# A planned attention + experts + relu-squared kernel: GpSimd takes a multiplication of VectorE, and the planner gets new costs and a new table of due times

## The chip, the cores and the metric

The kernel runs on one core of one Trainium2 chip. The metric is the device time of one execution in microseconds (us), the median of three runs; lower is better. The engines are named as in the profile: PE (TensorE matmul), PEld (its weight loads), DVE (VectorE), ACT (ScalarE), POOL (GpSimd), SP (SyncE, which issues most DMAs).

## What is computed

Three layers follow each other. All inputs and outputs are float32.

```python
# attention: 2 batches, 8 heads, 576 positions, 64 wide; window of 128 back
scores = scale * np.matmul(q, k.transpose(0, 1, 3, 2))
bias = slopes[:, None, None] * (-np.abs(rel))[None, :, :]
scores = np.where(mask, scores + bias[None], -1e9)
attn = softmax(scores)                      # rows, with + 1e-09 in the divisor
x = np.matmul(attn, v)                      # then (1152, 512)
# four experts, weighted by the normalised domain probabilities
p = domain_probs / (domain_probs.sum(-1, keepdims=True) + 1e-09)
for e in range(4):
    out += p[:, e:e + 1] * (np.maximum(x @ w1[e], 0.0) @ w2[e])     # 512 -> 1024 -> 512
# a last layer
h = np.maximum(x @ w_in, 0.0)               # 512 -> 2048
return h * h @ w_out
```

## The kernel before

**Work and precision.** Most matmuls run on operands split in two: a rounded part (`xh`, `wh`, `qh`, `kh`) and the rest (`xl`, `wl`, `ql`, `kl`), three products in place of one. A rounding is a copy into the rounded type (`rounded`, L555 on ACT, L557 on DVE); a rest is a subtraction (`rest`, L561, on POOL or DVE).

**Units.** Attention is cut into units of two heads. The first four units (`u` 0 to 3, "raw") are the first 128 positions of both batches and use plain float32; later ones cover 256 or 192 positions of one batch. Each unit goes through a chain of stages named in the table of due times: `sc` (scores, PE L908/L922/L931), `jo` (join the mask, DVE L949), `mx` (add the bias, find the maximum, DVE L969), `ex` (exponential, ACT L979, four squares in a raw unit), `in` (sum and reciprocal, DVE L986 and L990), `no` (normalise, DVE L995, ACT L1002 or POOL L1008), `tp` (transpose, PE L1018), `hi` (copy out of PSUM, L555 or L557), `ow`/`be` (mask both halves, POOL L1039), and then `pv` (attention times v, PE L798 for the raw units, L812 later) and its evacuation: `evx` (raw units, into `xfirst`), `evh` and `evl` (rounded part and rest of `x`).

**First expert meanwhile.** The first expert's first product (`g1`: PE L1901 in plain float32 for the first positions, L1103 later) and second product (`g2`: L1852, L1343) are interleaved with the attention units, item by item, with the roundings and rests of its weights (`wh`, `wlo` in the table).

**What sets the order.** All of this up to about 120 us is a static plan. `Plan.add` records a task: the engines it may use with occupancy and latency, what it depends on, which buffers it takes, and a due time, to which the table `LATER` adds a number by the task's name. `Plan.run` then plays the tasks against a small model of five engines and emits them: it takes the engine that can start earliest, and of the tasks ready on it the one due first. The order in which it emits is the order of each engine's queue on the chip. The model charges an overlap of DVE and POOL: `HELD` lengthens the POOL side, `SLOWED` times the overlap lengthens a DVE task that is marked `shared`. Where PE would sit idle in the first microseconds, `keep_busy` (L588) fills the modelled gap with small matmuls on zeros, the `pad` rows.

**What the change touches there.** `build_bias` (L650 on ACT, L654 on DVE) makes the position bias of two heads, for the own block and for the block before it: eight tasks in all, each of which the model puts on DVE or ACT. `norm_probs` (L1086 to L1088) normalises the domain probabilities `pt`, 128 x 9 x 4 numbers: sum, reciprocal, multiplication, all on DVE; the first user is the evacuation of the first expert. `where`/`ENGINE` in the kernel before put the `hi` of unit 0 on ACT.

After the plan the rest of the program (experts 1 to 3 and the last layer, PE L1223 and L1317) is emitted by other code with its own bookkeeping, and the change leaves that code alone.

Of the kernel before, what the change touches and what calls it, by code (L numbers as in the profile page):

```python
# [28 lines left out]

LATER = {  # L30
# [18 lines left out]
class Plan:  # L49
# [12 lines left out]
    SLOWED = 0.3  # L62
# [8 lines left out]
    def add(  # L71
        self, name, opts, fn, deps=(), takes=(), bufs=(), due=0.0, follow=(), cold=True,
        shared=False
    ):
        t = dict(
            name=name, opts=opts, fn=fn, deps=[d for d in deps if d], takes=list(takes),
# [29 lines left out]
    def run(self, until=None):  # L106
        todo = self.tasks
        while todo and not (until and until()):
# [23 lines left out]
            if other and (eng == "POOL" or eng == "DVE" and t["shared"]):  # L132
# [3 lines left out]
                else:  # L136
                    both = min(occ, max(end - start, 0.0))
                    more = self.SLOWED * both
# [19 lines left out]
def kernel(  # L158
# [363 lines left out]
    ENGINE = {("hi", 0): "ACT"}  # L522

    def where(key, u, opts):

        return [x for x in opts if x[0] == ENGINE.get((key, u), x[0])]

# [148 lines left out]
    def unit_tasks(u, due):  # L676
# [80 lines left out]
        if not raw:  # L757
            tqh = add("qh", [act(G * nq), dve(G * nq)], qh, shared=True, deps=[lq], takes=[b_["qh"]],
                      bufs=[b_["rq"]], due=first - 9.0)
            tkh = add("kh", [act(G * nk), dve(G * nk)], kh, shared=True, deps=[lk], takes=[b_["khl"]],  # L760
# [93 lines left out]
        if raw:  # L854
            add("evx", where("evx", u, [act(nb * nq), dve(nb * nq)]), evx, deps=[tpv], bufs=[b_["work"]],
                due=end - 0.9)
            teh = add("evh", [act(nb * nq), dve(nb * nq)], xh_later, shared=True,
# [9 lines left out]
    def job_tasks(u, i, t, add, b_, end, ready, G, q0, k0, pos, wide):  # L867
# [22 lines left out]
        def stage(name, opts, fn, lag, **kw):  # L890
            opts = where(name, u, opts)
            mine[name] = add(key + name, opts, fn, due=end - lag - later, follow=[last.get(name)], **kw)
            return mine[name]
# [159 lines left out]
        tsc = stage("sc", [pe(us)], scores, 7.4, deps=ready + ([] if raw else [task["j0mx", x] for x in range(NP - 2, NP)]),  # L1053
# [6 lines left out]
        tmx = stage("mx", [("DVE", us, 0.38 if raw else us + 0.1)], top, 9.5 if raw else 6.4,  # L1060
# [1031 lines left out]
```

## Time and profile before

| | us |
|---|---|
| median of 3 runs | 638.15 (637.5 to 638.3) |
| the profiled execution | 637.58, its span 635.9 |
| PE busy | 630.1 (99%) |
| DVE busy | 473.5 (74%) |
| POOL busy | 377.5 (59%) |
| ACT busy | 301.5 (47%) |

The span runs from the first to the last instruction; the 1.7 us beside it lie around the program. Busy time of PE counts the pads too, and the ends of matmuls in it are modelled, so short waits between two matmuls can hide in it; the distance from one start to the next shows them.

### The profile page before, as it was taken

The page shows a single profiled execution, that of the slowest core. Times are in us where ns is not written, and L with a number is a line of the kernel's source. Part 1 is how long each engine was busy: PE and PEld are TensorE (multiplying, and loading weights), DVE is VectorE, ACT ScalarE, POOL GpSimd, SP SyncE. Part 2 cuts the span into 40 slices and gives each one's busy share as a digit, 9 for nine tenths or more (in the row PEclk, how much of TensorE's full clock was granted, in tenths as well). Part 3 has the DMA queues.
Part 4 walks back from the last instruction along what each step waited for, and adds up shares of the span by engine and source line. Part 5 has one row for each costly group of instructions (what it writes and reads, how often), then busy time and mean ns, then how long its engine had stood idle before and what let it go on. Part 6 is the DMA issues. An engine that isn't in the chain of part 4 may idle for free.

```text
span 635.9 us, 11035 instructions
## 1 busy us (share of the span) xinstructions
PE 630.1 (99%) x3918; PEld 565.0 (89%) x3918; DVE 473.5 (74%) x1027; ACT 301.5 (47%) x769; POOL 377.5 (59%) x487
## 2 busy tenths in 40 slices
PE   9999999999999999999999999999999999999997
PEld 7788889899998998998998998999999898998996
DVE  7899876388887777777777777668768767667463
ACT  8889866145444344334334444354554544343220
POOL 3597853089676446446447546246687776766531
PEclk9999999999999999999999999999999999999999
DMA  8953430222134434434434433311123223001012
GB/s 245 278 150 85 119 90 18 100 66 100 35 116 136 140 107 152 133 103 157 135 103 147 133 120 125 106 64 68 34 76 125 88 78 116 18 2 51 1 66 84
DMA packets 46983, 64.70 MB, mean 102 GB/s; under 512 B 6480, under 2 KB 29264, under 8 KB 46928
## 3 DMA queue, kind: packets, MB, share of 16 engines
q1 hardware_dynamic: 35520, 39.48, 20.2%
q10 hardware_dynamic: 11408, 24.51, 12.4%
q8 instruction: 31, 0.51, 0.3%
q14 instruction: 24, 0.20, 0.1%
HBM read 53.23 MB, written 10.75 MB: 101 GB/s over the span
## 4 chain that ended last, share of the span: by engine, by line
PE 96%; ACT 2%; DVE 1%; issue 0%; POOL 0%; POOLq 0%
PE yacc L1317 38%; PE hps L1223 35%; PE hps L1103 6%; PE yacc L1343 6%; PE xps L812 2%; PE sc L931 1%; PE tp L1018 1%; PE hps L1901 1%; PE yacc L1852 1%; ACT ts L979 1%; PE pad L588 1%; PE xtp L1409 1%; PE sc L922 1%; ACT wh L555 0%; PE xps L798 0%; ACT ts L1002 0%
## 5 line engine op out<-in xcount | busy, mean ns | idle before, releaser
L1317 PE MATMUL yacc<-wh,hmem 128*128 128x512 f32 x716 | 227.8, 390 | 0.0
L1317 PEld LDWEIGHTS yacc<-wh,hmem 128*128 128x128 f32 x716 | 134.5, 188 | 27.0
L1317 PE MATMUL yacc<-wl,hmem 128*128 128x512 f32 x358 | 139.7, 390 | 0.0
L561 POOL TENSOR_TENSOR wl<-wraw,wh 128x256 fp32r<-128x256 f32 (+1 forms) x80 | 77.0, 987 | 42.0 <-ACT wh L484 27.7
L561 POOL TENSOR_TENSOR hmem<-c,hmem 128x320 fp32r<-128x320 f32 (+1 forms) x64 | 59.2, 944 | 59.3 <-ACT hmem L1254 53.2
L561 POOL TENSOR_TENSOR ls<-wsum,hs 128x256 fp32r<-128x256 f32 x77 | 61.7, 828 | 54.3 <-ACT hs L429 53.6
L1234 ACT ACTIVATE p<-hps 128x256 f32<-128x256 f32 (+1 forms) x80 | 32.9, 411 | 108.2 <-PE hps L1223 108.1
L1238 DVE TENSOR_TENSOR u<-hps,p 128x256 f32<-128x256 f32 (+1 forms) x80 | 36.5, 456 | 64.0 <-PE hps L1223 61.7
L1317 PEld LDWEIGHTS yacc<-wl,hmem 128*128 128x128 f32 x358 | 67.3, 188 | 12.6
L561 POOL TENSOR_TENSOR la<-wraw,ha 128x256 fp32r<-128x256 f32 x54 | 49.0, 928 | 17.3 <-ACT ha L415 17.3
L322 DVE SCALAR_TENSOR_TENSOR wconv<-wraw,wconv 128x512 int32<-128x512 int32 x64 | 58.0, 906 | 1.3
L1258 ACT ACTIVATE hmem<-c 128x256 fp32r<-128x256 f32 (+1 forms) x72 | 31.2, 446 | 53.0 <-DVE c L1238 51.4
L1259 DVE SCALAR_TENSOR_TENSOR hmem<-c,hmem 128x256 fp32r<-128x256 f32 (+1 forms) x72 | 42.8, 615 | 14.2 <-ACT hmem L1258 13.2
L1254 ACT ACTIVATE hmem<-c 128x320 fp32r<-128x320 f32 (+1 forms) x64 | 27.3, 446 | 52.2 <-DVE c L1248 33.5
L405 POOL TENSOR_TENSOR wsum<-wraw 128x256 f32<-128x256 f32 x37 | 31.0, 837 | 22.0 <-PE hps L1103 14.4
L1343 PE MATMUL yacc<-wh,hmem 128*128 128x512 f32 x128 | 43.4, 395 | 0.0
L1363 DVE SCALAR_TENSOR_TENSOR y<-yacc,pt,y 128x512 f32<-128x512 f32 x54 | 37.2, 738 | 0.3 <-PE yacc L1317 0.3
L302 ACT ACTIVATE wconv<-wraw 128x512 f32<-128x512 f32 x32 | 21.4, 670 | 30.8 <-DVE wconv L322 27.6
L1223 PE MATMUL hps<-ht,ls 128*128 128x320 f32 (+1 forms) x160 | 34.4, 297 | 0.4 <-POOL ls L561 0.4
L1039 POOL TENSOR_SCALAR_AFFINE_SELECT pt<-pt 128x256 f32<-128x256 f32 (+1 forms) x64 | 28.5, 454 | 10.5 <-ACT pt L555 6.6
L1103 PE MATMUL hps<-xh,wh 128*128 128x256 f32 (+1 forms) x112 | 34.6, 309 | 0.0
L1223 PE MATMUL hps<-xh,hs 128*128 128x320 f32 (+1 forms) x160 | 34.6, 297 | 0.0
(163 smaller groups left out, 1555.9 us busy)
## 6 DMA issues: line engine op xcount, KB each, us to landing
wraw<-in_w_dram SPq DMA_DIRECT2D x32, 512.0 KB, 3.7
wraw<-in_w_out_dram ACTq DMA_DIRECT2D x16, 512.0 KB, 3.9
w<-wconv ACTq DMA_DIRECT2D x32, 256.0 KB, 3.9
wraw<-w SPq DMA_DIRECT2D x16, 512.0 KB, 3.2
wraw<-in_w_in_dram ACTq DMA_DIRECT2D x14, 512.0 KB, 3.7
rq<-in_qT_dram SPq DMA_DIRECT2D x8, 256.0 KB, 7.8
out_dram<-y SPq DMA_DIRECT2D x7, 256.0 KB, 2.1
rk<-in_kT_dram SPq DMA_DIRECT2D x8, 192.0 KB, 5.5
```

The source lines that it names most:

```text
L322: nc.vector.scalar_tensor_tensor(out=ai, in0=raw[j][:, :, part], scalar=amount, in1=ai, op0=op, op1=ALU.bitwise_or,)
L405: e_.tensor_tensor(out=t["s"][:, o:o + 2, :], in0=x(), in1=y(), op=op)
L561: e.tensor_tensor(out=out, in0=in0, in1=f32(in1), op=ALU.subtract)
L1103: nc.tensor.matmul(out=ps, lhsT=l_[:, k, cs], rhs=r_[:, k, cols], start=(k == 0 and r_ is xh and l_ is wh and not second), stop=(k == KT - ...
L1223: nc.tensor.matmul(out=ps, lhsT=a[l_][:, k, :], rhs=b[r_][:, k, :], start=start and (k, l_, r_) == (0, 0, 0), stop=stop and (k, l_) == (1, ...
L1234: nc.scalar.activation(out=out, in_=x, func=ACTF.Copy)
L1238: nc.vector.tensor_tensor(out=out, in0=x, in1=y, op=ALU.add)
L1258: nc.scalar.activation(out=hh, in_=src, func=ACTF.Relu)
L1259: nc.vector.scalar_tensor_tensor(out=hl, in0=src, scalar=0.0, in1=f32(hh), op0=ALU.max, op1=ALU.subtract)
L1317: nc.tensor.matmul(out=y, lhsT=l_[:, ns], rhs=r_[:, fo, cols], start=(first and fo == 0 and j == 0), stop=(last and fo == FTQ - 1 and j == 2),
L1343: nc.tensor.matmul(out=y, lhsT=l_[:, ns], rhs=r_[:, fo, :], start=(first and j == 0), stop=(last and j == 2),)
L1363: nc.vector.scalar_tensor_tensor(out=yt, in0=y, scalar=pt[:, nt, e:e + 1], in1=yt, op0=ALU.mult, op1=ALU.add)
```

## The change

It moves the multiplication of the domain probabilities to GpSimd as a task of its own, changes costs in the planner, replaces the pin of `hi` by a table `ENGINE` by task name, and replaces the table `LATER` whole.

```diff
+ENGINE = {
+    "bias": "ACT", "wlo1.1": "POOL", "j0no15": "ACT",
+}
 LATER = {
-    "j1be8": 8, "j0mx16": 9, "j0sc17": 8, "lk4": -4, "j1tp4": -8, "j1sc4": -2, "hh22": -1,
...
+    "lk17": -1, "qh16": 8, "lk6": -8, "g1.0": 3, "ql8": -2, "j1sc12": 4, "j1mx11": -2,
...
-    SLOWED = 0.3
+    SLOWED = {True: 0.3, "copy": 1.0}
...
-            name=name, opts=opts, fn=fn, deps=[d for d in deps if d], takes=list(takes),
+            name=name, opts=[x for x in opts if x[0] == ENGINE.get(name, x[0])], fn=fn, deps=[d for d in deps if d], takes=list(takes),
...
-                    more = self.SLOWED * both
+                    more = self.SLOWED[t["shared"]] * both
...
-    ENGINE = {("hi", 0): "ACT"}
-    def where(key, u, opts):
-        return [x for x in opts if x[0] == ENGINE.get((key, u), x[0])]
...
-            tqh = add("qh", [act(G * nq), dve(G * nq)], qh, shared=True, deps=[lq], takes=[b_["qh"]],
+            tqh = add("qh", [act(G * nq), dve(G * nq)], qh, shared="copy", deps=[lq], takes=[b_["qh"]],
```

The tasks `kh`, `evh` (raw) and `wh` get `shared="copy"` in the same way.

```diff
-        tsc = stage("sc", [pe(us)], scores, 7.4, deps=ready + ([] if raw else [task["j0mx", x] for x in range(NP - 2, NP)]),
+        tsc = stage("sc", [("PE", us, us + 0.06) if raw else pe(us)], scores, 7.4, deps=ready + ([] if raw else [task["j0mx", x] for x in range(NP - 2, NP)]),
...
-        tmx = stage("mx", [("DVE", us, 0.38 if raw else us + 0.1)], top, 9.5 if raw else 6.4,
+        tmx = stage("mx", [("DVE", us, 0.28 if raw else us + 0.1)], top, 9.5 if raw else 6.4,
...
     def norm_probs(eng):
         nc.vector.tensor_reduce(out=psum_p, in_=probs_sum, axis=mybir.AxisListType.X, op=ALU.add)
         nc.vector.reciprocal(out=psum_p, in_=psum_p)
-        nc.vector.tensor_tensor(
+
+
+    def share_probs(eng):
+        nc.gpsimd.tensor_tensor(
             out=pt, in0=pt, in1=psum_p.unsqueeze(2).to_broadcast([P, NTILE, E]), op=ALU.mult
         )
...
-                    opts = [("ACT", 0.7, 4.05 if b else 3.9)]
+                    opts = [("ACT", 0.7, 3.85)]
...
-    t_np = plan.add("np", [("DVE", 0.9, 1.0)], norm_probs, deps=[t_pt], due=60.0)
+    t_np = plan.add("np", [("DVE", 0.42, 0.5)], norm_probs, deps=[t_pt], due=59.0)
+    t_np = plan.add("sp", [("POOL", 0.3, 0.35)], share_probs, deps=[t_np], due=60.0)
```

**ACT, from its first instruction** (`bias` is `build_bias`, `ts` with `st` the exponentials of a unit, `pt<-tp` the copy `hi`, `xfirst` the evacuation `evx`). Before:

```order
L1719 DMA first<-in_kT_dram 128x2x128 x2
L650 ACT_TABLE_LOAD
L650 ACTIVATE bias<-rel 128x128 x8
L979 ACTIVATE ts,st_98<-ts,st_98 128x128 x4
L979 ACTIVATE ts,st_99<-ts,st_99 128x128 x4
L979 ACTIVATE ts,st_100<-ts,st_100 128x128 x4
L555 ACTIVATE pt<-tp 128x512
L979 ACTIVATE ts,st_101<-ts,st_101 128x128 x4
```

Now:

```order
L1720 DMA first<-in_kT_dram 128x2x128 x2
L650 ACT_TABLE_LOAD
L650 ACTIVATE bias<-rel 128x128 x16
L978 ACTIVATE ts,st_98<-ts,st_98 128x128 x4
L978 ACTIVATE ts,st_99<-ts,st_99 128x128 x4
L978 ACTIVATE ts,st_100<-ts,st_100 128x128 x4
L555 ACTIVATE xfirst<-xps 128x256
L978 ACTIVATE ts,st_101<-ts,st_101 128x128 x4
```

All 16 bias instructions stand ahead of the first exponential, where eight stood; the eight others were on DVE. The copy of unit 0 after its transpose has left ACT.

**DVE, raw units 1 to 3** (`st_99`, `st_100`, `st_101` are the sums of units 1, 2, 3). Before, after the maxima of unit 3:

```order
L557 COPY pt<-tp 128x512
L557 COPY xfirst<-xps 128x256
L986 TENSOR_REDUCE st_100<-st_100 128x4
L990 RECIPROCAL st_100<-st_100 128x4
L986 TENSOR_REDUCE st_101<-st_101 128x4
L990 RECIPROCAL st_101<-st_101 128x4
L995 TENSOR_TENSOR ts<-ts,st_100 128x512
L995 TENSOR_TENSOR ts<-ts,st_101 128x512
```

Now, after the maxima of unit 2, and so ahead of those of unit 3:

```order
L557 COPY pt<-tp 128x512
L985 TENSOR_REDUCE st_99<-st_99 128x4
L989 RECIPROCAL st_99<-st_99 128x4
L994 TENSOR_TENSOR ts<-ts,st_99 128x512
L985 TENSOR_REDUCE st_100<-st_100 128x4
L989 RECIPROCAL st_100<-st_100 128x4
```

and after the maxima of unit 3:

```order
L557 COPY pt<-tp 128x512
L557 CAST xh<-xfirst 128x256
L985 TENSOR_REDUCE st_101<-st_101 128x4
L989 RECIPROCAL st_101<-st_101 128x4
L557 COPY xfirst<-xps 128x256
L994 TENSOR_TENSOR ts<-ts,st_101 128x512
```

DVE now copies out both first transposes, does the sum and the product of unit 1 behind the first copy, and no longer multiplies unit 2, which POOL takes.

**DVE around the domain probabilities** (`psum_p`; `xl<-xps` is the rest `evl` of a pair of units). Before:

```order
L557 CAST qh<-rq 128x512
L1086 TENSOR_REDUCE psum_p<-pt 128x9
L1087 RECIPROCAL psum_p<-psum_p 128x9
L1088 TENSOR_TENSOR pt<-pt,psum_p 128x9x4
L561 TENSOR_TENSOR khl<-rk,khl 64x768
L949 COPY_PREDICATED sc<-below,sc 128x2x128
L561 TENSOR_TENSOR xl<-xps,xh 128x2x256
```

Now:

```order
L557 CAST xh<-xps 128x2x256
L985 TENSOR_REDUCE st_102<-st_102 128x2
L989 RECIPROCAL st_102<-st_102 128x2
L561 TENSOR_TENSOR xl<-xps,xh 128x2x256
L557 CAST qh<-rq 128x512
L1085 TENSOR_REDUCE psum_p<-pt 128x9
L1086 RECIPROCAL psum_p<-psum_p 128x9
```

The rest of the pair now stands ahead of the rounding and the sums that stood ahead of it, and the multiplication is gone from DVE; it stands on POOL between two masks of `pt`.

## Rows read from the trace of the kernel before

**Rows 1.** The profile's page, part 1: busy us, share, instructions.

```profile
PE 630.1 (99%) x3918; PEld 565.0 (89%) x3918; DVE 473.5 (74%) x1027; ACT 301.5 (47%) x769; POOL 377.5 (59%) x487
```

**Rows 2.** Busy time by stretch; after POOL: PEclk, DMA share, GB/s.

```profile
40.00:60.00 20.00, 19.30 (x138) 16.31 (x138) 19.18 (x61) 17.75 (x58) 16.58 (x17) 1.00 0.43 119
...
120.00:636.00 516.00, 512.20 (x2984) 464.37 (x2982) 378.50 (x667) 211.65 (x473) 305.32 (x359) 1.00 0.29 93
```

**Rows 3.** Waits of PE from 12.3 to 130 us: total, times, longest.

```profile
PE hps L1103 <- DVE xl L561: 0.6, 1, 0.6
```

**Rows 4.** Timeline of ACT: start, us, instruction, idle before and releaser.

```profile
3.16 1.71 ACT L650 ACTIVATE bias<-rel 128x128 bf16<-128x128 f32 x8
5.65 0.40 ACT L979 ACTIVATE ts<-ts,st 128x128 f32<-128x128 f32 x1 [0.78 <-DVE st L969]
...
10.28 0.58 ACT L555 ACTIVATE pt<-tp 128x512 f32<-128x512 f32 x1
...
24.00 0.68 ACT L1002 ACTIVATE ts<-ts,st 128x128 f32<-128x128 f32 x2
```

**Rows 5.** Timeline of DVE, raw units.

```profile
7.33 0.16 DVE L986 TENSOR_REDUCE st<-st 128x4 f32<-128x8 f32 x1 [0.24 <-ACT ts L979]
...
7.73 0.69 DVE L995 TENSOR_TENSOR ts<-ts,st 128x512 f32<-128x512 f32 x1
8.34 0.28 DVE L969 CUSTOM_DVE_ANT_0 ts<-sc,bias 128x128 f32<-128x128 f32 x1
...
9.19 0.15 DVE L986 TENSOR_REDUCE st<-st 128x4 f32<-128x8 f32 x1
...
11.09 0.69 DVE L557 COPY pt<-tp 128x512 f32<-128x512 f32 x1
```

**Rows 6.** Timeline of PE, raw units.

```profile
8.57 0.63 PE L1018 MATMUL tp<-ident,ts 128*128 128x128 f32 x4 [0.30 <-ACT ts L979]
9.04 1.45 PE L588 MATMUL pad<-idle 128*128 128x128 bf16 x23
...
10.98 0.66 PE L798 MATMUL xps<-pt,first 128*64 128x128 f32 x8
...
14.66 0.63 PE L1018 MATMUL tp<-ident,ts 128*128 128x128 f32 x4
...
16.43 0.66 PE L798 MATMUL xps<-pt,first 128*64 128x128 f32 x8
...
24.68 0.38 PE L1018 MATMUL tp<-ident,ts 128*128 128x128 f32 x2
```

**Rows 7.** Timeline of DVE around the domain probabilities.

```profile
47.67 1.24 DVE L557 CAST qh<-rq 128x512 fp32r<-128x512 f32 x1
...
49.30 1.09 DVE L1088 TENSOR_TENSOR pt<-pt,psum_p 128x36 f32<-128x36 f32 x1
...
51.88 0.69 DVE L561 TENSOR_TENSOR xl<-xps,xh 128x512 fp32r<-128x512 f32 x1
```

**Rows 8.** Timeline of POOL at the same time.

```profile
49.04 1.30 POOL L561 TENSOR_TENSOR ql<-rq,qh 128x512 fp32r<-128x512 f32 x1 [0.42 <-PE tp L1018]
```

**Rows 9.** Timeline of PE: the stretches from one start to the next.

```profile
51.76 0.28 PE L1103 MATMUL hps<-xh,wh 128*128 128x256 f32 x1
52.62 0.39 PE L1103 MATMUL hps<-xl,wh 128*128 128x256 f32 x1 [0.58 <-DVE xl L561]
...
58.04 0.28 PE L931 MATMUL sc<-khl,ql 128*128 128x256 f32 x1
58.35 0.44 PE L1018 MATMUL tp<-ident,ts 128*128 128x128 f32 x2
58.88 0.38 PE L931 MATMUL sc<-khl,qh 128*128 128x256 f32 x1
```

**Rows 10.** Groups by form, 0 to 130 us: busy, mean ns, idle before.

```profile
L1008 POOL TENSOR_SCALAR ts<-ts,st 128x128 f32<-128x128 f32 x27 | 11.9, 450 | 9.4 <-ACT ts L979 5.6 <-DVE st L986 1.2 <-PE sc L931 1.0
...
L557 DVE CAST wh<-wraw 128x512 fp32r<-128x512 f32 x2 | 1.0, 485 | 0.0
```

More of the change, by code (lines that the diff above doesn't have):

```diff
@@ L757, in unit_tasks @@
         if not raw:
-            tqh = add("qh", [act(G * nq), dve(G * nq)], qh, shared=True, deps=[lq], takes=[b_["qh"]],
+            tqh = add("qh", [act(G * nq), dve(G * nq)], qh, shared="copy", deps=[lq], takes=[b_["qh"]],
                       bufs=[b_["rq"]], due=first - 9.0)
-            tkh = add("kh", [act(G * nk), dve(G * nk)], kh, shared=True, deps=[lk], takes=[b_["khl"]],
+            tkh = add("kh", [act(G * nk), dve(G * nk)], kh, shared="copy", deps=[lk], takes=[b_["khl"]],
                       bufs=[b_["rk"]], due=first - 9.1)
@@ L854, in unit_tasks @@
         if raw:
-            add("evx", where("evx", u, [act(nb * nq), dve(nb * nq)]), evx, deps=[tpv], bufs=[b_["work"]],
+            add("evx", [act(nb * nq), dve(nb * nq)], evx, deps=[tpv], bufs=[b_["work"]],
                 due=end - 0.9)
-            teh = add("evh", [act(nb * nq), dve(nb * nq)], xh_later, shared=True,
+            teh = add("evh", [act(nb * nq), dve(nb * nq)], xh_later, shared="copy",
                       deps=[task["evx", u]], due=end + 6.0)
@@ L890, in stage @@
         def stage(name, opts, fn, lag, **kw):
-            opts = where(name, u, opts)
             mine[name] = add(key + name, opts, fn, due=end - lag - later, follow=[last.get(name)], **kw)
@@ L1804, in weight_parts @@
                 f"wh{i}.{h}", [act(m), dve(m)], lambda eng, h=h: hi(eng, h),
-                shared=True, deps=[t] + room_, due=later - 4.0 + h,
+                shared="copy", deps=[t] + room_, due=later - 4.0 + h,
                 follow=[wtask.get(("hi", i, 0))],
```

15 rows, old and new, of the table LATER are left out of this document.

## The prediction

> **What bounds the kernel now.** I read the busy shares first. PE is busy for 99% of the span [rows 1], so the kernel takes as long as PE's own work plus the few microseconds in which PE has none. The table of stretches says where those can be: from 120 us on PE is busy for 512.2 of 516 us, most of the rest being the tail after its last matmul, and from 40 to 60 us for 19.3 of 20, while DVE is busy for 19.18 there, more than in any other engine's list [rows 2]. After 120 us the change leaves every queue in the same order, and the granted clock is 1.00, the 2.4 GHz level, in both stretches. So the change can act in two ways alone: by the moment at which the raw units let PE run without gaps, and by the short waits up to 120 us in which DVE is late. The view of waits names one such wait of PE, 0.6 us for a rest `xl` from DVE [rows 3]; since ends of matmuls are modelled I took the others from the distance between starts. Between 51.76 and 52.62 us lie 0.86 us for a matmul whose neighbours take 0.12, between 58.04 and 58.35 us 0.31, and between 58.35 and 58.88 us 0.53 for two transposes of about 0.1 each [rows 9].
>
> The sum is made against the profiled execution, 637.58 us, of which 635.9 is the span; the median of the three runs shown is 638.15, 0.57 more, and I put the sum on the median. About 0.2%, 1.28 us, is what a measurement of this kernel can tell from no change.
>
> **The change part by part.**
>
> *The bias on ACT.* Now ACT makes eight bias instructions in 1.71 us from 3.16 us on and then sits idle for 0.78 us until the first exponential at 5.65, which waits for the first maximum on DVE [rows 4]. Sixteen take 3.42 us and end at 6.58, so the first exponential starts 0.93 us later. On DVE the eight were made before the first scores existed, so nothing is won there. What follows the exponential follows it: the sum at 7.33, the transpose at 8.57 us [rows 5, 6] become 8.26 and 9.50.
>
> *The copy of unit 0 on DVE.* Now it is queued on ACT behind the exponentials of three units and starts at 10.28, more than 1 us after its transpose [rows 4, 6]. On DVE it stands behind the maxima of unit 2: those take 8.34 to 9.19 us now [rows 5], so 9.27 to 10.12, then the copy with its 0.69 [rows 5], to 10.8. The first attention product can start at about 10.95 us, where it starts at 10.98 now [rows 6]: the lateness of ACT is made good for unit 0. The price is paid by the next units. Sum and product of a unit take 0.40 and 0.61 on DVE (7.33 to 7.73 to 8.34) [rows 5]. Unit 1's product now starts 0.40 after 9.19, at 9.59; it will start at 10.75 + 0.40 = 11.15. Then come the sum of unit 2 (to 12.16), the maxima of unit 3 (to 13.0), the second copy (to 13.65). The exponentials of unit 3 start 0.3 after its first maximum, 12.5, and a unit needs 1.68 from its first exponential to its sum (5.65 to 7.33) [rows 4, 5], so that sum stands at 14.2. After it DVE evacuates unit 1 (an estimate of 0.35, half the wide copy) and multiplies, 14.95 to 15.55. The transpose of unit 3 follows at about 15.7, against 14.66 now [rows 6]: 1.05 us later. The last attention product of the raw units comes 1.77 us behind that transpose now (16.43) [rows 6], and PE's order between them stays (attention product of unit 2, one `g1` instruction, attention product of unit 3). I take **+1.05**. Below, PE may have fed on other work for part of it: +0.6. Above, the product of unit 3 can be stretched by a POOL subtraction that runs beside it, by its own length at most: +1.65.
>
> *The product of unit 2 on POOL*: four instructions of 0.45 [rows 10], 1.8 us from about 12.2 us on, ready at 14.0 at the latest; PE asks for that transpose behind the second attention product, at about 14.4. So it costs nothing; without that cover it would be worth the difference of 0.4 at most.
>
> *Nine pads fewer* (84 to 75). A pad in that gap takes 1.45 / 23 = 0.06 us [rows 6], so 0.57 us less; but they stand in a gap that the copy of unit 0 ends, so they are worth nothing either way.
>
> *The domain probabilities.* On DVE the multiplication of 36 numbers a row took 1.09 us, from 49.30 to 50.39; a POOL subtraction ran from 49.04 to 50.34 [rows 7, 8]. Ahead of it a rounding took 1.24 us where others took 0.485 on average [rows 7, 10]. Both stand ahead of the `xl` that starts at 51.88 [rows 7] and for which PE waits. By the Trainium skill ("SBUF — State Buffer", Who interferes with whom) a GpSimd instruction and a VectorE one with two SBUF inputs exclude each other for the whole of an instruction, and the row agrees: the multiplication ended 0.05 us after POOL's. By that rule the same multiplication on GpSimd can lock DVE out in its turn, but only for its own length. I price the multiplication on POOL between nothing and 1.09 us and take 0.45, the nearest POOL row [rows 10]; POOL is busy for 16.6 of 20 us there [rows 2], and no PE instruction needs its result before the first expert is evacuated, so what it delays is the masks behind it. Now the `xl` of the pair stands ahead of rounding and sums. I take the 0.74 us (0.86 less 0.12) as gone.
>
> *The rest of the table.* The two waits at 58 us (0.19 and 0.33) [rows 9] come from the same DVE backlog, which is 1.09 + 0.8 us shorter; I take them as gone too: **-1.26** in all. Other orders bring other waits. DVE's queue keeps about the same work in the plan (five instructions fewer, two more roundings), so one wait of the kind at 58 us is likely: **+0.3**. Bounds: none, and 1.2, as much as there is now. The new factor for roundings and the other new costs of the planner change no duration, only the order; they are in these terms.
>
> Sum: +1.05 - 1.26 + 0.3 = +0.1, so 638.25, **638.3 us**.
>
> **The rivals.**
>
> *ACT stays behind (slower).* At 24.68 us a pair of transposes starts at the moment at which ACT ends their normalisation (24.00 + 0.68) [rows 4, 6]: no margin. ACT now has 1.71 us of bias more ahead of it, 0.58 + 0.41 of copies less, and normalises 32 squares in place of 29, at 0.34 each (0.68 / 2). If ACT is then later than PE's own 1.05, each transpose behind a normalisation waits, and these waits take the place of DVE's. Price: +1.05, +1.0 for three more normalisations, and of the gain only the 0.74: +1.3 or a little more, 639.6 us. It decides where ACT's lateness at the first transposes of the later units passes PE's. For it: no margin there now. Against it: ACT is busy for 17.75 of 20 us at 40 to 60 us [rows 2] and can catch up.
>
> *Roundings block in full (slower).* One rounding beside POOL took 1.24, the two `wh` 0.485 [rows 7, 10]. If all eight of the plan's roundings on DVE are held as that one was, 0.75 each, and two of them stand ahead of a rest that PE waits for, the gain is lost again: +0.1 + 1.5 = +1.6, 639.8 us. The rule of the page named above would have it so for roundings between two SBUF tiles; the two short ones speak against it.
>
> *The start costs less and all waits go (faster).* +0.6 in place of +1.05, no new wait, and 0.6 of waits around 18 us that are too short for the rows: -1.3, 636.9 us. For it: the planner's costs are nearer to the rows. Against it: the 0.93 on ACT has nowhere to hide.
>
> **How the numbers follow.** Forecast 0.58; ACT behind 0.18; roundings 0.08; faster 0.16. Faster by over 0.2% needs -1.28, the far end of the last case, and I give it 0.14. Slower by over 0.2% is both slower cases, 0.26 less the part of them that stays under 1.28, plus the upper end of the forecast: 0.25. Within 0.2%: 0.61. The range: low, the faster case, 636.8; high, +1.65 with half the gain and one wait more, about +2, 640.1. One case in ten at each end lies outside.
>
> **What would show it.** In the profile of the changed kernel: the bias on ACT ends at 6.6 us and the first exponential starts there; the first transpose of the raw units at 9.5, the first attention product still near 11.0, the transpose of unit 3 at 15.7, and the last product 1.0 us later than 16.43. PE has no wait for `xl` near 52 us, and the multiplication on POOL is under 0.5 us. It is wrong if the first exponential still starts at 5.7, if the last raw product is not late, or if PE shows new waits for ACT between 20 and 65 us that add up to more than 1 us.

## The result, and the profile after

| | before | changed |
|---|---|---|
| median, same chip | 638.2 us (637.5 to 638.3, 4 runs) | 641.76 us (641.61 to 642.73, 4 runs) |
| ratio | | 1.0061, 95% interval 1.0044 to 1.0079 |
| profiled execution, span | 635.9 us | 641.0 us |

The changed kernel is slower by 3.6 us, more than the 0.2% that a measurement can tell from no change. The forecast was 638.3 us with a range of 636.8 to 640.1 us: wrong, and outside the range. The profiled execution of the changed kernel is its longest (the spans of its other three runs are 639.8, 639.9 and 640.0 us), that of the kernel before about its shortest: the two profiles lie 5.1 us apart, the medians 3.6.

The page's busy times hardly moved [rows 1]: PE works as long as before, so what was added is time in which it waits.

```profile
PE 631.8 (99%) x3909; PEld 564.9 (88%) x3909; DVE 476.9 (74%) x1022; ACT 301.5 (47%) x775; POOL 373.9 (58%) x489
```

First, where the time came in. From some 120 us on all queues are the same, so a matmul there is a common point of both programs. It stands here in the timeline of PE, first of the kernel before, then of the changed one:

```profile
131.55 0.39 PE L1343 MATMUL yacc<-wh,hmem 128*128 128x512 f32 x1
```

```profile
136.69 0.39 PE L1344 MATMUL yacc<-wh,hmem 128*128 128x512 f32 x1
```

It comes 5.14 us later, and the rest of the span is the same in both (504.3 us). The last attention product of the raw units splits these 5.14: it starts at 16.43 us before [rows 6] and at 18.19 now, so **1.76 us** belong to the start, and **3.38 us** to the stretch from there to the common point (115.12 us before, 118.50 now). The timeline of PE of the changed kernel shows what the stretch is made of:

```profile
18.19 0.66 PE L798 MATMUL xps<-pt,first 128*64 128x128 f32 x8
...
19.35 1.46 PE L1902 MATMUL hps<-xfirst,wraw 128*128 128x256 f32 x6
21.29 0.70 PE L1902 MATMUL hps<-xfirst,wraw 128*128 128x256 f32 x2 [0.47 <-ACT hfirst L1836]
...
22.30 1.46 PE L1902 MATMUL hps<-xfirst,wraw 128*128 128x256 f32 x6
23.59 0.38 PE L1017 MATMUL tp<-ident,ts 128*128 128x128 f32 x2
23.81 1.46 PE L1902 MATMUL hps<-xfirst,wraw 128*128 128x256 f32 x6
25.75 1.13 PE L1902 MATMUL hps<-xfirst,wraw 128*128 128x256 f32 x4 [0.47 <-ACT hfirst L1836]
...
36.27 0.28 PE L930 MATMUL sc<-khl,ql 128*128 128x256 f32 x1
36.71 0.62 PE L1017 MATMUL tp<-ident,ts 128*128 128x128 f32 x2 [0.16 <-ACT ts L1001]
37.08 0.36 PE L1104 MATMUL hps<-xh,wh 128*128 128x256 f32 x1
...
46.98 0.28 PE L930 MATMUL sc<-khl,ql 128*128 128x256 f32 x1
47.82 0.62 PE L1017 MATMUL tp<-ident,ts 128*128 128x128 f32 x2 [0.57 <-ACT ts L1001]
48.20 0.48 PE L1344 MATMUL yacc<-wh,hmem 128*128 128x512 f32 x1
...
49.45 0.40 PE L1344 MATMUL yacc<-wh,hmem 128*128 128x512 f32 x1
50.20 0.39 PE L930 MATMUL sc<-khl,qh 128*128 128x256 f32 x1 [0.36 <-DVE st L968]
...
50.66 0.28 PE L930 MATMUL sc<-khl,ql 128*128 128x256 f32 x1
51.09 0.39 PE L930 MATMUL sc<-khl,qh 128*128 128x256 f32 x1
...
59.68 0.29 PE L1104 MATMUL hps<-xh,wl 128*128 128x256 f32 x1
59.81 0.38 PE L1017 MATMUL tp<-ident,ts 128*128 128x128 f32 x2
59.94 0.36 PE L930 MATMUL sc<-khl,qh 128*128 128x256 f32 x1
...
104.64 0.28 PE L1104 MATMUL hps<-xh,wl 128*128 128x256 f32 x1
105.20 0.62 PE L1017 MATMUL tp<-ident,ts 128*128 128x128 f32 x2 [0.28 <-ACT ts L1001]
105.58 0.36 PE L930 MATMUL sc<-khl,qh 128*128 128x256 f32 x1
```

Read it by distances from start to start:

- Six hps instructions take 1.29 us (22.30 to 23.59) but 1.94 twice, at 19.35 and 23.81: 0.65 each, **1.3 us**, a wait for ScalarE's copy `hfirst`.
- From the instruction before a pair of transposes to the one behind it are 0.26 us without a wait (59.68 to 59.94), and 0.81, 1.22 and 0.94 at 36.27, 46.98 and 104.64: 0.55, 0.96 and 0.68, **2.2 us**, each time a wait for the normalisation on ScalarE.
- Scores wait for maxima on VectorE: 0.75 and 0.43 us where 0.23 and 0.12 are usual, **0.8 us**.

With some 0.3 us for a transpose at 98.97 us that is 4.6 us. The waits of before, for `xl` at 52.62 and around 58 us [rows 9], are gone: 1.26 us. What is left, some 3.3 us, is nearly all of the stretch's 3.38.

Who is late? The view of waits puts it to ScalarE (1.0 and 0.9 us), where before it named only `xl` [rows 3]:

```profile
PE tp L1017 <- ACT ts L1001: 1.0, 3, 0.6
PE hps L1902 <- ACT hfirst L1836: 0.9, 2, 0.5
PE tp L1017 <- DVE ts L994: 0.9, 1, 0.9
PE sc L930 <- DVE st L968: 0.4, 1, 0.4
```

But ScalarE's own timeline has idle time ahead of the normalisation of 47.37 us, waiting for VectorE's sum:

```profile
3.15 3.30 ACT L650 ACTIVATE bias<-rel 128x128 bf16<-128x128 f32 x16
6.35 0.39 ACT L978 ACTIVATE ts<-ts,st 128x128 f32<-128x128 f32 x1
...
20.85 0.38 ACT L1836 ACTIVATE hfirst<-hps 128x256 f32<-128x256 f32 x1 [1.12 <-PE hps L1902]
...
47.37 0.69 ACT L1001 ACTIVATE ts<-ts,st 128x128 f32<-128x128 f32 x2 [1.21 <-DVE st L989]
```

And in VectorE's timeline that sum (46.93) stands behind a subtraction of 1.89 us, which ran beside the key subtraction on GpSimd (second fence):

```profile
14.65 1.62 DVE L994 TENSOR_TENSOR ts<-ts,st 128x512 f32<-128x512 f32 x1
...
36.33 0.95 DVE L557 CAST wh<-wraw 128x512 fp32r<-128x512 f32 x2
...
43.85 1.89 DVE L561 TENSOR_TENSOR wl<-wraw,wh 128x512 fp32r<-128x512 f32 x1
...
46.93 0.14 DVE L985 TENSOR_REDUCE st<-st 128x2 f32<-128x4 f32 x1
...
102.12 2.14 DVE L561 TENSOR_TENSOR khl<-rk,khl 64x640 fp32r<-64x640 f32 x1
```

```profile
14.45 1.27 POOL L561 TENSOR_TENSOR ql<-rq,qh 128x512 fp32r<-128x512 f32 x1
...
35.96 1.04 POOL L1038 TENSOR_SCALAR_AFFINE_SELECT pt<-pt 128x256 f32<-128x256 f32 x2 [1.68 <-DVE st L985]
...
43.02 2.17 POOL L561 TENSOR_TENSOR khl<-rk,khl 64x768 fp32r<-64x768 f32 x1
...
61.73 0.25 POOL L1090 TENSOR_TENSOR pt<-pt,psum_p 128x36 f32<-128x36 f32 x1
```

So the theory after the result: the new order puts VectorE's sums behind subtractions that GpSimd stretches, and ScalarE and TensorE wait in turn. The rival is that of the prediction: ScalarE is behind by its own work. And the two waits for `hfirst` need an explanation of their own.

### The profile page after: what moved, and what is told of

Read it like the earlier page. It is cut to its first block, busy times and chain, and to the rows that moved or that the text cites. A ratio compares the mean times of both kernels' runs of the same rounds, so it can differ in the third digit from the quotient of the medians.

```text
span 641.0 us, 11022 instructions
## 1 busy us (share of the span) xinstructions
PE 631.8 (99%) x3909; PEld 564.9 (88%) x3909; DVE 476.9 (74%) x1022; ACT 301.5 (47%) x775; POOL 373.9 (58%) x489
## 4 chain that ended last, share of the span: by engine, by line
PE 92%; DVE 3%; DMA 2%; ACT 1%; issue 1%; POOL 0%; SPq 0%; DVEq 0%; ACTq 0%; POOLq 0%
PE yacc L1318 38%; PE hps L1224 35%; PE yacc L1344 6%; PE hps L1104 6%; PE xps L812 2%; PE sc L930 1%; DMA wraw<-in_w_dram 1%; PE hps L1902 1%; PE tp L1017 1%; DVE khl L561 1%; PE xtp L1410 1%; DVE wl L561 1%; DVE ts L968 1%; DMA first<-in_kT_dram 0%; PE sc L921 0%
## 5 line engine op out<-in xcount | busy, mean ns | idle before, releaser
L1038 POOL TENSOR_SCALAR_AFFINE_SELECT pt<-pt 128x256 f32<-128x256 f32 (+1 forms) x64 | 26.7, 422 | 20.7 <-ACT pt L555 11.7
L1224 PE MATMUL hps<-ht,hs 128*128 128x320 f32 (+1 forms) x160 | 34.5, 297 | 0.0
```

The source lines that it names most:

```text
L1224: nc.tensor.matmul(out=ps, lhsT=a[l_][:, k, :], rhs=b[r_][:, k, :], start=start and (k, l_, r_) == (0, 0, 0), stop=stop and (k, l_) == (1, ...
```

## The experiments

All are set against runs of the kernel before on their own chip (medians 638.26 to 638.64 us); ratios stand with their 95% intervals. "Stretch" is the time from the last raw attention product to the common point in the profiled execution, 115.12 us before and 118.50 changed.

| run | edit | median us | ratio to before | stretch us |
|---|---|---|---|---|
| changed | | 641.76 | 1.0061 (1.0044 to 1.0079) | 118.50 |
| e1 | bias back on VectorE | 641.47 | 1.0046 (1.0034 to 1.0059) | 118.35 |
| e2 | multiplication back on VectorE | 641.88 | 1.0060 (1.0046 to 1.0074) | 118.68 |
| e3 | three pieces held | 641.47 | 1.0047 (1.0035 to 1.0060) | 118.46 |
| e5 | one `ql` on VectorE | 641.55 | 1.0050 (1.0036 to 1.0064) | 118.45 |
| e8 | one `wl` on GpSimd | 640.89 | 1.0038 (1.0026 to 1.0051) | 117.37 |
| e9 | e8 and two VectorE moves | 639.82 | 1.0023 (1.0014 to 1.0032) | 116.52 |
| e10 | e9, e1 and e3 | 640.44 | 1.0031 (1.0019 to 1.0042) | 116.65 |
| e13 | e9, e3 and keys first | 639.20 | 1.0013 (1.0004 to 1.0022) | 115.93 |
| e14 | e13 and e5 | 638.93 | 1.0010 (1.0002 to 1.0019) | 116.06 |
| p1 | factor for roundings 0.3 | 640.91 | 1.0043 (1.0029 to 1.0056) | |
| p2 | old table and pin | 639.35 | 1.0020 (1.0011 to 1.0029) | |
| p6 | factors swapped | 641.63 | 1.0054 (1.0040 to 1.0068) | |
| e4 | before, multiplication on GpSimd | 637.77 | 0.9988 (0.9979 to 0.9997) | |
| e12 | before, bias on ScalarE | 638.53 | 1.0001 (0.9992 to 1.0010) | |

### The multiplication: e4 and e2

In the kernel before, alone (e4):

```diff
-        nc.vector.tensor_tensor(
+        nc.gpsimd.tensor_tensor(
             out=pt, in0=pt, in1=psum_p.unsqueeze(2).to_broadcast([P, NTILE, E]), op=ALU.mult
```

> The kernel before with only the multiplication of the domain probabilities moved to GpSimd, every other instruction in its place. My theory: the 1.09 us on VectorE go, the rest xl starts about 1 us earlier, TensorE's gap of 0.74 us before 52.62 us is gone, the two transposes near 58 us wait 0.2 to 0.5 us less, and the total falls by 0.7 to 1.2 us. Rival: the multiplication on GpSimd stands between two subtractions there, makes the masks and the second one late and locks VectorE out for as long; the gap stays or moves to a later transpose, total the same within 0.3 us.

Measured: 0.84 us less by the medians, and the interval excludes no change, if narrowly. PE's timeline of e4 has 0.11 us between the matmuls that stood 0.86 apart, but the two waits near 58 us are still there, 0.31 and 0.53 us from start to start as before [rows 9]:

```profile
52.85 0.28 PE L1103 MATMUL hps<-xh,wh 128*128 128x256 f32 x1
52.96 0.28 PE L1103 MATMUL hps<-xl,wh 128*128 128x256 f32 x1
...
59.48 0.29 PE L931 MATMUL sc<-khl,ql 128*128 128x256 f32 x1
59.78 0.44 PE L1018 MATMUL tp<-ident,ts 128*128 128x128 f32 x2
60.31 0.39 PE L931 MATMUL sc<-khl,qh 128*128 128x256 f32 x1
```

The profiled execution is e4's longest (639.03 us; its raw units wait for late loads of keys), so the gain stands in the medians and not in this profile.

The multiplication took 1.02 us on GpSimd, beside the key subtraction on VectorE, which kept its 0.95:

```profile
51.34 1.02 POOL L1088 TENSOR_TENSOR pt<-pt,psum_p 128x36 f32<-128x36 f32 x1 [0.73 <-DVE psum_p L1087]
```

e4 is the version that beats both kernels, by a small margin over the one before. In the changed kernel the move was undone (e2, the opposite edit):

> The changed kernel with only the multiplication of the domain probabilities back on VectorE, in its place in the program (among the maxima near 58 us). My theory: VectorE's sums there come later by the 0.7 to 1.1 us of the multiplication, and the transposes and scores between 58 and 66 us wait for part of that; the total rises by 0.3 to 1.1 us over the changed kernel. Rival: in this order the multiplication stands where VectorE has room (TensorE has no wait between 52 and 90 us), and the total is the same within 0.3 us, so the move to GpSimd is worth nothing in the changed order.

Measured: no difference from the changed kernel, so the rival holds. In that order the multiplication meets no subtraction on GpSimd and takes VectorE 0.19 us (minimum, median and maximum in ns of the one instruction, in the view of its line):

```profile
L1090 DVE TENSOR_TENSOR pt<-pt,psum_p x1: 189/189/189, 62.1 to 62.1; 128x36 f32<-128x36 f32 x1
```

So the move is worth 0.8 us in the old order and nothing in the new one: the wait for `xl` went with the order.

### The bias: e1 and e12

e1 undoes the pin in the changed kernel, e12 makes it alone in the kernel before:

```diff
-                lambda eng, c=c, own=own: build_bias(c, own, eng),
+                lambda eng, c=c, own=own: build_bias(c, own, "DVE" if own else eng),
```

> The changed kernel with the eight bias instructions of the tiles' own columns back on VectorE, ahead of the first scores; all other queues as in the changed kernel. My theory: ScalarE's sixteen bias instructions hold the first exponential only from 6.06 (first maximum 5.77 + 0.29) to 6.35 us, so the first exponential starts 0.3 us earlier and so do the sum at 8.02, the first transpose at 9.27 and the transpose of unit 3 at 16.42; the total falls by 0.3 us at most. Rival, the step of the prediction: the bias on ScalarE costs the whole of its lateness, and the transpose of unit 3 comes at 15.5 or earlier, 0.9 us sooner or more. Second rival: the product of unit 3 still runs beside the subtraction on GpSimd and eats the 0.3 us: total unchanged.

```diff
-                lambda eng, c=c, own=own: build_bias(c, own, eng),
+                lambda eng, c=c, own=own: build_bias(c, own, "ACT"),
```

> The kernel before with only the eight bias instructions of VectorE moved to ScalarE, every other instruction in its place. My theory: ScalarE's sixteen end at 6.35 to 6.45 us and hold the first sum at 8.0 us or later (7.33 before, when the first scores came early); TensorE is 0.4 to 0.7 us later at the transpose of unit 0 and of unit 3, and the total is 0.3 to 0.7 us over the kernel before where the first loads come early, nothing where they come late. Rival, the step of the prediction: 0.93 us later at the first exponential, and about 1 us of total.

Measured: e12 is the same as before, and e1 the same as the changed kernel within the intervals. e12's profiled execution had its first maximum at 5.47 us and yet its first sum at 8.04, where 2.02 us lie between the two in the kernel before (5.31, 7.33):

```profile
5.47 0.29 DVE L969 CUSTOM_DVE_ANT_0 ts<-sc,bias 128x128 f32<-128x128 f32 x1 [3.00 <-PE sc L908]
...
8.04 0.16 DVE L986 TENSOR_REDUCE st<-st 128x4 f32<-128x8 f32 x1 [0.79 <-ACT ts L979]
```

So ScalarE's sixteen do hold the first sum at 8.0 us when the scores come early. But the first maximum moves from run to run, from 5.31 to 6.29 us in the profiled executions; e1, without the bias on ScalarE, had it at 6.16 and its sum at 8.18. What moves it is TensorE's clock. The loads that the first scores read had landed by 4.64 to 4.77 us in all sixteen profiled executions, but the 16 scores themselves took 1.16 us in the changed kernel and 2.08 us in e8, where the order up to there is the same:

```profile
4.90 1.16 PE L907 MATMUL sc<-first 64*128 64x128 f32 x16
```

```profile
4.91 2.08 PE L907 MATMUL sc<-first 64*128 64x128 f32 x16
```

In both, the small pads ahead of the scores start 0.107 us apart and most of those behind them 0.056, which are the 1.2 and 2.4 GHz levels. The clock rose ahead of the scores in the one (the trace's first record of a granted clock of 1.00 is at 4.86 us) and at their end in the other (7.03 us). PE had run the same 35 pads ahead of the scores in both, so what lets the clock rise earlier in one execution stays open. Over many runs nothing of the 0.7 us is left. The prediction's profile was one of the early ones: 637.58 us, where the lowest of 73 later runs of that kernel is 637.66.

### The product of unit 3: e5

From here on, edits to the changed kernel are made where the plan issues a task, so that all other queues stay as they are: HOLD issues a piece of a task (counted from 0) behind another task, PIN gives it another engine.

```diff
-            t["fn"](eng)
+            emit(self, t, eng)
...
+HOLD = {}
+PIN = {("ql4", 0): "DVE"}
```

> The changed kernel with the first query subtraction (ql of unit 4) on VectorE behind the product of unit 3, in place of GpSimd. My theory: the product of unit 3 took 1.62 us because that subtraction ran beside it; alone it takes 0.69, the transpose of unit 3 starts at about 15.5 in place of 16.42, the last attention product of the raw units at 17.3 in place of 18.19, and the total falls by 0.7 to 1.0 us (the key subtraction behind it is 0.2 us earlier or later, which does not count). Rival: the product is long for another reason, 1.6 us still: the total is the same or 0.7 us longer, by the subtraction that VectorE now has to make.

Measured: the product of unit 3 takes 0.68 us, the last raw product starts at 17.04 us, but the total did not fall as expected: the median is that of e1 and e3, which made no such edit and had a product of 0.68 too. The 1.62 us of the changed kernel's profile are a matter of the run: there GpSimd starts `ql` 0.20 us ahead of the product (14.45, 14.65). In e1 and e3 it starts 0.03 us behind it, and then the key subtraction that follows is the long one, 1.92 us, for which nothing waits. What is won is steadiness: five spans within 0.3 us (639.7 to 640.0), against 639.8 to 641.0 for the changed kernel.

### The waits for `hfirst`: e3

```diff
+HOLD = {("g1.1", 3): "j1sc4", ("g1.3", 2): "j0sc5", ("g1.3", 3): "j0sc5"}
```

> The changed kernel with three of TensorE's hps pieces issued behind the next group of scores: the fourth of item 1 and the third and fourth of item 3. My theory: the two gaps before 21.29 and 25.75 us are waits for the relu copy that reads the shared tile of the pair, 0.6 us each; behind a group of scores they are covered, TensorE is 1.0 to 1.2 us ahead of the changed kernel at 29 us, and the total falls by 0.9 to 1.2 us. Rival: VectorE's backlog (three subtractions of keys between 23.5 and 26.4 us) sets the time there anyway; the gaps come back before the next scores or transposes, and the total is the same within 0.3 us.

Measured: of the two waits 0.2 us is left, and the stretch is what it was. The rival holds: 0.9 us came back at the next scores (0.90 us behind the piece before them, where 0.03 is usual), which then waited for a key subtraction (VectorE's row holds two; the first of them ended at 24.31 us, 0.14 us before the scores start, while the `hfirst` that the PE row names was not what they read), the rest in smaller steps:

```profile
24.45 0.36 PE L930 MATMUL sc<-khl,qh 128*128 128x256 f32 x1 [0.52 <-ACT hfirst L1836]
```

```profile
22.26 3.12 DVE L561 TENSOR_TENSOR khl<-rk,khl 64x768 fp32r<-64x768 f32 x2
```

### VectorE's late sums: e8, e9, e10

```diff
+HOLD = {("wlo0.0", 0): "kl8"}
+PIN = {("wlo0.0", 0): "POOL"}
```

> The changed kernel with one subtraction of weights (the 1.89 us at 43.85 us on VectorE, beside the key subtraction on GpSimd) made on GpSimd behind that key subtraction. My theory: the normalisation on ScalarE at 47.37 us was late because VectorE's sum before it was, and VectorE was late by this stretched subtraction; the sum comes 1.2 to 1.5 us earlier, TensorE's gaps before 47.82 and 48.12 us (0.95 us) are gone and those before 50.2 and 51.09 us (0.85 us) shrink; the total falls by 0.9 to 1.8 us. Rival, the one of the prediction: ScalarE itself is behind; it has no idle time before that normalisation, the gaps stay, and the total is the same within 0.3 us.

```diff
+HOLD = {("wlo0.0", 0): "kl8", ("j1hi5", 0): "j1in6", ("kl19", 0): "j1in17"}
+PIN = {("wlo0.0", 0): "POOL"}
```

> The changed kernel with three instructions of VectorE moved: the subtraction of weights of 43.85 us on GpSimd as in the run before, the copy of probabilities at 35.47 us behind the two sums that follow it, and the key subtraction at 102.12 us (2.14 us beside GpSimd) behind the two sums that follow it. My theory: the waits of TensorE for ScalarE's normalisations are all waits for a sum that stands behind a subtraction on VectorE; the gaps at 36.71 and 37.0 us shrink by 0.3 us, those at 47.82 to 51.09 us are gone, those at 105.2 and 105.49 us (0.65 us) are gone; the total is 1.4 to 2.4 us under the changed kernel, 639.3 to 640.3 us. Rival, ScalarE behind by its own work: the gaps at 36 and 105 us stay, and the total is that of the run before, 640.9 us.

Measured: e8 takes 1.1 us off the stretch, and e9 another 0.85. In e8 PE has no wait for the maxima near 50 us any more and 0.4 us of the 0.96 for the transposes, but waits 0.3 us for VectorE near 62 us instead. The normalisation of 47.37 us comes at 46.10 in e8, still waiting for VectorE and not held up by ScalarE's own work:

```profile
46.10 0.69 ACT L1001 ACTIVATE ts<-ts,st 128x128 f32<-128x128 f32 x2 [0.61 <-DVE st L989]
```

In e9, which came out in the range expected, the key subtraction takes 0.82 us where it took 2.14, and the transposes at 105 us do not wait. Near 36 us 0.2 us is left of 0.55, and near 47 us 0.5, before which ScalarE again stands idle (0.80 us) for VectorE. Nothing was taken from ScalarE in either run, so ScalarE behind by its own work is ruled out for the waits that went. The stretched time moves as well: in e8 the next subtraction, `ql`, took 1.89 us in the place of `wl`, but VectorE had one subtraction less.

e10 has the diffs of e9, e1 and e3 together:

> The changed kernel with all edits found so far that take work out of a wait: the three VectorE moves of the run before, the bias of the own columns on VectorE, and the three hps pieces behind scores. My theory: the waits that are left are those of the start (0.7 us) and one for a key subtraction near 24.5 us (0.7 us), so TensorE is 1.0 to 1.8 us behind the kernel before at 120 us and the total is 639.0 to 640.0 us, still not faster than before. Rival: each wait taken away lets another come up, and the total stays at 640.5 us or more.

Measured: the stretch of e9 and no better median, above the range expected and close to the rival; holding the pieces without the keys is worth nothing, as in e3, and the bias nothing, as in e1.

### Keys first: e13, e14

```diff
+HOLD = {
...
+    ("j0in4", 0): "kl5", ("j1jo4", 0): "kl5", ("j0no4", 0): "kl5", ("j1mx4", 0): "kl5",
+}
```

> The changed kernel with the three VectorE moves of the run e9, the three hps pieces behind scores, and the key subtraction of unit 5 on VectorE ahead of the first sum of unit 4 (GpSimd's normalisation of unit 4 stays behind that sum). My theory: holding the pieces alone won nothing because the next scores then waited for that key subtraction, which was long beside GpSimd; made while GpSimd and VectorE are idle (21.2 to 22.0 us) it takes 0.95 us, the wait near 24.5 us is gone, TensorE between 18 and 30 us falls back by 0.2 us at most where it fell back by 1.2 us, and the total is 0.8 to 1.2 us under that of e9: 638.6 to 639.0 us. Rival: a third thing is late there (the queries' subtraction on GpSimd, the normalisation), and the total is that of e9, 639.8 us.

e14 adds the PIN of e5:

> As e13, and the first query subtraction on VectorE behind the product of unit 3. My theory: in about half of the runs GpSimd starts that subtraction before the product of unit 3, which then takes 1.62 in place of 0.69 us, and the last raw product comes 1.0 us later; without it no run has that, the spans lie within 0.6 us of each other, and the median is that of e13's shorter runs, 638.2 to 638.8 us. Rival: the two spans 1 us apart come from the landing of the first loads; then e14 shows them too.

Measured: the key subtraction runs while GpSimd is idle and takes 0.95 us, and the scores that waited at 24.45 us in e3 follow without a gap at 23.96 us:

```profile
20.40 0.95 DVE L561 TENSOR_TENSOR khl<-rk,khl 64x768 fp32r<-64x768 f32 x1
```

The stretch falls by 0.6 us against e9 and the median by as much, less than the 0.8 expected: a pair of transposes behind GpSimd's normalisation is now 0.2 us late, and the held pieces still wait 0.16 us twice. So the loss near 21 and 26 us had two layers, the shared tile and behind it VectorE's keys: holding the pieces alone won nothing (e3, e10), and with the keys first it won 0.6 us. The keys first without the pieces held was not run. e14's spans lie within 0.8 us (636.9 to 637.7) where e13's spread over 1.9 (636.6 to 638.5): this agrees with the collision of `ql` and the product as the source of much of the spread, but the one profile of e13 has no collision, so it is not shown. The median lies just above the range expected. Together the edits win back 5 of the 6 thousandths; both stay slower than the kernel before.

### The plan's parts: p1, p2, p6

```diff
-    SLOWED = {True: 0.3, "copy": 1.0}
+    SLOWED = {True: 0.3, "copy": 0.3}
```

> The changed kernel with the planner's factor for roundings beside GpSimd set back to 0.3; the plan makes its order anew from the same table of due times, and PE's order differs in some 500 rows. My theory: the factor is not what costs, since roundings were not stretched in either trace; the new order has waits of its own of the same size, and the total is within 1.5 us of the changed kernel's 641.7, on either side. Rival: counting the roundings in full made the plan push VectorE's work together, and without it the total comes back to 638.2 to 639.5 us.

p2 has the table and the pin of the kernel before in place of the new ones:

```diff
-    "bias": "ACT", "wlo1.1": "POOL", "j0no15": "ACT",
+    "j0hi0": "ACT",
```

> The changed kernel with the table of due times and the one pin of the kernel before (the unit-0 copy on ScalarE, bias left to the plan); the new costs and the multiplication on GpSimd stay. My theory: the table and the costs belong together, so the old table under the new costs gives an order with new waits: 639.5 to 642.5 us. Rival: the new table alone carries the loss, and the old one brings back the time before less the multiplication: 637.0 to 638.5 us.

```diff
-    SLOWED = {True: 0.3, "copy": 1.0}
+    SLOWED = {True: 1.0, "copy": 0.0}
```

> The changed kernel with the planner's two factors the other way round: subtractions on VectorE beside GpSimd counted at full overlap, roundings at none, as the two traces show them (subtractions up to 2.1 us where 0.7 to 0.95 is the time alone, roundings 0.42 to 0.69 beside GpSimd and 0.42 to 0.55 alone); the order is made anew from the same table. My theory: a plan that expects the long subtractions puts them where they hold up less, and the total is under the changed kernel: 639.0 to 641.2 us. Rival: the table was made for the other factors, and the new order has as many waits: 641.2 to 643 us.

Measured: with the old table the ratio is 1.0020, clear of the changed kernel's interval, so most of the loss goes with the new table and its pins. The order that the old table gives under the new costs has waits of its own (1.2 us for a normalisation on GpSimd before 43.66 us). The new table under the old costs was not run, so table and costs are not told apart beyond that. p1 cannot be told from the changed kernel by its interval. p6, in which I had expected the plan to do better, does not: its new order has other waits (one of 1.6 us, before the transpose at 89.75 us, for a copy on VectorE). Both expectations took roundings as not stretched, which leaves out the 1.24 us of the kernel before [rows 7]. What a right factor would be worth with a table made for it was not tried.

## Why the prediction was wrong, step by step

- **The multiplication and the 0.74 us: right in the old order.** e4 won 0.84 us. The price on GpSimd was 0.45, between the 0.25 us of the changed kernel and the 1.02 of e4. In the changed kernel the multiplication adds nothing to what the new order does: e2.
- **"I take them as gone too: -1.26 in all": right in the number, by another cause.** None of the three waits is there. But the two near 58 us were put down to the same backlog of VectorE, shorter by the multiplication, and e4, which takes the multiplication alone away, keeps both (0.31 and 0.53 us from start to start). The new order removed them.
- **The start, +1.05: luck at best.** It was added up from the bias (0.93 us at the first exponential) and from the work that VectorE takes over with the first copy. The first exponential starts at 6.35 us, not 6.6, and the bias alone costs nothing in the median (e12). The transpose of unit 3 does come near the 15.7 us forecast where nothing collides (15.27 to 15.77 in e1, e3, e5, e8, e13 and e14). But the 14.66 of the kernel before that it was set against is that of an early execution: with the same raw units it starts at 15.73 in e4, which waited for loads of keys, and with the bias moved at 15.37 in e12. In e1, e3 and e5 the medians lie 2.9 us above the kernel before, less than the 3.2 to 3.3 by which their stretch is longer, so at the median the start costs nothing that these runs can tell. The profiled execution lost 1.76 us, above the bound of 1.65, by the case that the bound was set for: the product of unit 3 stretched to 1.62 us by the subtraction beside it.
- **"Other orders bring other waits ... +0.3. Bounds: none, and 1.2": this is the step that failed.** The new waits are 4.6 us. I priced them as one wait of the kind at 58 us, with the old total as the upper end, because VectorE's list was about as long. But what counts is where the stretched subtractions stand, not the length of the list: with the new table the 1.89 us at 43.85 and the 2.14 us at 102.12 stand ahead of sums that ScalarE and TensorE wait for, and e9 won back more than half of the stretch's loss by moving three instructions. The prediction's own sign of being wrong came with it: PE's waits for ScalarE between 20 and 65 us add up to 1.7 us (0.47, 0.47, 0.16 and 0.57). Also missed: the second item of a pair writes the tile that `hfirst` reads. Before, four scores stood between the two; in the new order nothing does. That could be read from the order beforehand.
- **The rival "ACT stays behind": right symptom, wrong cause, and too cheap.** Transposes do wait for normalisations on ScalarE between 36 and 105 us, as it said. But ScalarE was idle for 1.21 us before the longest. Its 639.6 us lacked the waits for `hfirst` and for the maxima.
- **"Roundings block in full": the mechanism holds, the price did not fall due.** A rounding between two SBUF tiles that starts while a GpSimd subtraction is under way is held until that ends. In the order of the kernel before the rounding of 1.24 us [rows 7] comes again in e12 (1.24), e4 (1.23) and p2 (1.34), each time some 0.28 us past the end of GpSimd's `wl`, where 0.41 is the time alone. Here it is in e4:

```profile
49.67 1.23 DVE L557 CAST qh<-rq 128x512 fp32r<-128x512 f32 x1
```

```profile
48.90 1.72 POOL L561 TENSOR_TENSOR wl<-wraw,wh 128x512 fp32r<-128x512 f32 x1
```

  The two short roundings that the prediction set against it ran beside masks and normalisations of GpSimd, pieces of some 0.4 us, as did those of 0.95 us together in the changed kernel (36.33), so they spoke for nothing. In the changed order no such rounding starts beside a subtraction under way, so the rival's 1.5 us is not in the loss. The Trainium skill ("SBUF — State Buffer", Who interferes with whom) names both kinds: an instruction of VectorE with two inputs in SBUF contends with GpSimd's reads, and copies and casts can contend in a two-port mode. The rows agree with both halves (subtractions 0.69 to 1.89 and 0.82 to 2.14 us, roundings 0.41 to 1.24).

## What to carry to other kernels

When a planner's order changes as a whole, the time it gives depends on which short instruction stands behind which stretched one; walk the new order at each place where TensorE takes a result (a transpose, a group of scores, the second half of a shared tile) and ask what stands ahead of it on the engine behind the engine that the wait will name. Try a good local edit in the old order too: here the multiplication alone beats both kernels, and the rest of the change hid it. And take the start of a kernel from several runs, since one profile can be early or late by as much as the term in question (the last raw product of the kernel before at 16.43 us, and at 17.48 in e4, whose raw units are the same).

## What the runs showed of the hardware

- One small instruction, a product of 36 numbers a row, took 0.19 us on VectorE and 0.25 on GpSimd where the other engine had no subtraction, but 1.09 us on VectorE beside a GpSimd subtraction [rows 7, 8] and 1.02 on GpSimd beside a VectorE subtraction: four to six times as long.
- In these rows a VectorE instruction whose inputs all lie in SBUF, started while a GpSimd subtraction was under way, ended a fixed time past it: products and subtractions of 128x512 0.55 us (the 1.62 and the 1.89 us above), the roundings 0.28 us. The 2.14 us at 102.12 spans two GpSimd subtractions in a row. The rest `xl`, which reads `xps` from PSUM, kept its 0.69 us beside a GpSimd subtraction (51.88 us in the kernel before [rows 7], with `wl` on GpSimd from 51.75 us).
- 0.2 us in the start of one GpSimd subtraction decides whether VectorE's product (1.62 us, PE 1 us late) or the subtraction behind it (1.92 us, nobody late) is the long one. Of nine profiled executions with that pair in the changed order of the raw units, the four in which the first record of the full clock comes at 4.48 to 5.39 us had the long product (1.48 to 1.70 us for e9, e10, e2 and the changed kernel), and the five with it at 5.66 to 7.03 us had not (0.68): there an earlier clock went with a longer run. p1, whose order differs a little behind it, had the full clock at 4.13 us and no long product, so this is no rule; that the clock is what decides was not tried by itself.
